# Attention and mixture of experts on one core: another order of the block products of experts 1 to 7, with old and new layer-2 steps among them

## The chip, the cores and the metric

The kernel runs on one core of a Trainium2 chip. The metric is the device time of one execution in microseconds (us), median over runs.

## The reference

An attention (8 batches, 8 heads, 576 positions, head width 64; scores below the row's maximum less tau are masked out) gives 4608 rows x of 512 numbers. They go to a mixture of 8 experts:

```python
logits = x @ w_gate
noisy_logits = logits + np.log1p(np.exp(x @ w_noise)) * noise
top2 = np.argpartition(-noisy_logits, 2, axis=1)[:, :2]
...                                    # top2_w: softmax over the two logits
for e in range(E):
    for k in range(2):
        mask = top2[:, k] == e
        h = np.maximum(x[mask] @ w1[e], 0.0)
        out[mask] += top2_w[mask, k, None] * (h @ w2[e])
```

w1 is 8 x 512 x 1024, w2 is 8 x 1024 x 512, all fp32.

## The kernel before

Attention and routing fill the first part, with expert 0's first two groups of tokens among them. This document is about what follows, `run` (L1370): expert 0's third group, then experts 1 to 7, each of at most 1188 tokens in two halves, `phase(e, 0, ...)` with 640 tokens and `phase(e, 1, ...)` with 548.

Every matmul is done in three, since both operands are split into a rounded part and a rest (hi and lo, both fp32r): hi x hi, hi x lo, lo x hi. Each split costs a rounding on ScalarE (hi) and a subtract on VectorE (lo).

**Layer 1 of a half** is computed in 28 block products instead of 32, by the scheme that multiplies 2x2 blocks with seven products. For each of four units u (two of the eight blocks of the hidden width) there are the products k = 1 to 7; the 28 pairs (k, u) stand in the table `STEPS`. A product (`product`, L1216) is six matmuls of 320 columns in half 0 and of 274 in half 1. The sums of weight blocks that the scheme needs are four additions on GpSimd (`w1sum`, L1103), those of the inputs are on VectorE (`xsum`, L1177). Products go to PSUM banks x (one of two, by u), y and z. `evict` (L1240) empties them: k = 1, 5, 6 a copy on ScalarE (L1248) to one of three SBUF tiles; k = 2, 3, 7 an add on VectorE to that tile (L1251), then a relu on ScalarE one step later (L1255) and a subtract on VectorE two steps later (L1256); k = 4 relu and subtract from the bank itself. Products 1, 6, 4 and 7 of a unit use the same bank x, so that each of them waits for the eviction of the one before.

**Layer 2 of a half** is built by `second_steps` (L1349) from steps of three matmuls. `plain` (L1293) is a tile of 128 tokens in eight steps of 128x512; its output is scaled by the gate into one of three y buffers (L1301, on VectorE) and scattered (L1019, on GpSimd). `wide2` (L1314) is the rest of half 1 (292 columns) in four quarters of eight steps: VectorE transposes a quarter from its bank (L1333), and after the fourth multiplies by the gates (L1337); ten scatters of 32 rows follow. Layer-2 steps use two PSUM banks in turn. Half 0 has five plain tiles, half 1 two and the wide block (in expert 7 five). Expert 0's third group has one plain tile and a wide block as well.

**The order** is written out by hand. `step` issues the matmuls of one step, then evictions that are due, then side work: `run` gives each piece of side work the number of the step that it goes behind, in a list for the products and one for the layer-2 steps. Each engine runs its instructions in that order. SyncE issues the weight loads (`w1load` L1098, `w2load` L1125), GpSimd the gathers of token rows (`gather2`), which are bounced through DRAM (`bounce2`), loaded as blocks (`load2`) and transposed on VectorE (`turn2`, L1175); `sums` then schedules the input sums (L1186), roundings (`xhi` L1205, ScalarE) and subtracts (`xlo` L1210). Weights are split by `w1hi` (L1118) and `w1lo` (L1122), `w2hi` (L1132) and `w2lo` (L1137). Four raw buffers (`q`) take the loads of both layers' weights. Layer-1 weights of units 0 and 1 for the next half 0 are split in half 1, those of units 2 and 3 at the head of half 0; all eight layer-2 weights are loaded and split in half 0. One scatter at most is issued after each step.

The steps of a half before:

```python
steps = first[:-1] + second[:4] + first[-1:] + second[4:]   # L1359
```

27 products, four layer-2 steps, product (4, 3), and the other layer-2 steps.

## Time and profile before

| | |
|---|---|
| time, median of 3 runs | 1633.54 us (1632.52 to 1637.58) |
| the profiled execution | 1635.43 us, span 1633.3 us |
| TensorE matmul (PE) | 1464.0 us, 90% |
| VectorE (DVE) | 1095.3 us, 67% |
| ScalarE (ACT) | 822.0 us, 50% |
| GpSimd (POOL) | 761.3 us, 47% |

Busy times are of the profiled execution. Matmuls overlap in the pipeline, so a row's duration is longer than its distance to the next one. The program's part of this document starts at 713.67 us with the wide block of expert 0; expert 1 starts at 741.61, and the last matmul is at about 1623 us. The names in the rows are of memory places (n_xr, n_p and so on), which are used by several buffers; the line tells which operation it is.

### The profile page before, as it was taken

To read this page: it belongs to the slowest core of one execution; us is meant where nothing else is said; L and a number is where in the kernel's file an instruction comes from. 1 tells how busy PE (TensorE), PEld (TensorE's weight loads), DVE (VectorE), ACT (ScalarE), POOL (GpSimd) and SP (SyncE) were. 2 spreads that over 40 slices of the span, in tenths; PEclk is the share of its full clock that TensorE was granted. 3 is DMA by queue.
4 is the path that set the end of the run, shared out by engine and by line. 5 is a ranking of instruction groups with operands and counts; after the bars stand their busy time and mean duration, and the time that the engine had idled before them with its cause. 6 is when DMAs were issued, how large, how long until landed. Compare 5 with 4: busy or idle time off the path is not lost. (4 is left out here: it accounts for less than half of the span.)

```text
span 1633.3 us, 27794 instructions
## 1 busy us (share of the span) xinstructions
PE 1464.0 (90%) x9086; PEld 1190.4 (73%) x9086; DVE 1095.3 (67%) x2879; ACT 822.0 (50%) x1727; POOL 761.3 (47%) x1129
## 2 busy tenths in 40 slices
...
GB/s 184 172 208 184 213 161 207 163 222 175 200 168 149 202 128 81 104 146 132 72 160 98 84 163 90 90 167 55 122 152 70 122 155 63 130 143 62 141 33 28
DMA packets 189281, 220.59 MB, mean 135 GB/s; under 512 B 64212, under 2 KB 112300, under 8 KB 188112
## 3 DMA queue, kind: packets, MB, share of 16 engines
...
## 5 line engine op out<-in xcount | busy, mean ns | idle before, releaser
L1019 POOL DMA_INDIRECT out<-n_y,sx x52 | 85.8, 1650 | 366.6 <-DVE n_y L1301 362.6
L295 ACT ACTIVATE e<-ns,nm 128x576 f32<-128x576 f32 x288 | 223.2, 775 | 40.6 <-DVE ns L293 37.6
L318 DVE SCALAR_TENSOR_TENSOR p<-ns,thr,e 128x576 f32<-128x576 f32 x256 | 223.3, 872 | 21.2 <-ACT thr L303 20.4
L293 DVE TENSOR_SCALAR_CACHE_REDUCE ns<-sp 128x576 f32<-128x576 f32 x288 | 214.3, 744 | 22.2 <-PE sp L282 18.0
L330 PEld LDWEIGHTS tp<-ident,p 128*128 128x128 f32 x1024 | 110.6, 144 | 99.5 <-ACT ot L402 23.1
L333 ACT ACTIVATE pt<-tp 128x512 f32<-128x512 f32 x256 | 151.1, 590 | 56.3 <-PE tp L330 55.3
L396 PE MATMUL tp<-pt,vt 128*64 128x256 f32 (+1 forms) x1024 | 176.5, 429 | 0.0
L330 PE MATMUL tp<-ident,p 128*128 128x128 f32 x1024 | 167.7, 286 | 0.0
L282 PE MATMUL sp<-ks,qh 128*128 128x288 f32 x496 | 159.6, 335 | 4.6 <-DVE ns L293 4.6
L1248 ACT ACTIVATE n_qr<-m_tp 128x320 f32<-128x320 f32 (+1 forms) x168 | 67.7, 407 | 164.8 <-DVE n_y L1301 84.3
L1232 PE MATMUL m_tp<-n_vt,n_pt 128*128 128x320 f32 (+1 forms) x364 | 96.2, 319 | 48.3 <-ACT n_qr L1248 41.6
L282 PE MATMUL sp<-ks,ql 128*128 128x288 f32 x496 | 138.4, 296 | 0.6 <-DMA ql<-loq 0.6
L1019 POOL DMA_INDIRECT out<-n_y,ix x60 | 97.7, 1629 | 82.7 <-DVE n_y L1337 68.2
L1232 PE MATMUL m_tp<-n_p,n_pt 128*128 128x274 f32 (+1 forms) x700 | 122.0, 313 | 6.2 <-ACT n_qr L1248 4.9
L210 POOL TENSOR_TENSOR lok<-kr,hik 128x640 fp32r<-128x640 f32 x31 | 57.3, 1847 | 139.7 <-ACT hik L209 128.3
L1232 PEld LDWEIGHTS m_tp<-n_p,n_pt 128*128 128x128 f32 x700 | 107.8, 200 | 9.7 <-ACT n_qr L1248 6.7
L1301 DVE TENSOR_SCALAR n_y<-m_sp,gw 128x512 f32<-128x512 f32 (+1 forms) x52 | 39.0, 749 | 108.6 <-PE m_sp L1311 108.6
L1232 PEld LDWEIGHTS m_tp<-n_vt,n_pt 128*128 128x128 f32 x364 | 67.4, 199 | 54.2 <-ACT n_qr L1248 45.2
L1251 DVE TENSOR_TENSOR n_qr<-m_tp,n_qr 128x320 f32<-128x320 f32 (+1 forms) x168 | 76.9, 458 | 42.1 <-PE m_tp L1232 40.8
L639 POOL DMA_INDIRECT slot_table<-pay,sl x80 | 88.2, 1102 | 33.6 <-DVE m_vt L879 16.4
L1205 ACT ACTIVATE n_vt<-n_qr 128x640 fp32r<-128x640 f32 (+1 forms) x42 | 29.5, 701 | 139.3 <-DVE n_qr L1186 139.3
L282 PEld LDWEIGHTS sp<-ks,qh 128*128 128x128 f32 x496 | 93.5, 189 | 6.5 <-DVE ns L293 4.6
...
## 6 DMA issues: line engine op xcount, KB each, us to landing
...
```

Source lines behind the costliest of these rows:

```text
L282: nc.tensor.matmul(o, q_, k_, start=(i == 0), stop=(i == len(parts) - 1))
L293: nc.vector.tensor_scalar(ns, sp[:, :, 0:HALF], -1.0 / math.sqrt(D), None, op0=ALU.mult, op1=ALU.min, accum_out=nm)
L295: nc.scalar.activation(e, ns, AF.Exp, bias=nm, scale=-1.0)
L318: nc.vector.scalar_tensor_tensor(p, ns, thr, e, op0=ALU.is_le, op1=ALU.mult, accum_out=ssum[n][:, c:c + 1])
L330: nc.tensor.transpose(tp[:, kt, :], p[:, 128 * kt:128 * kt + 128], ident)
L333: nc.scalar.activation(pt[n][:, s, :, c0:c0 + 128], tp, AF.Copy)
L396: nc.tensor.matmul(o[64 * s:64 * s + 64, 0:c1 - c0], w, x, start=(kt == 0), stop=(kt == 4))
L639: st = nc.gpsimd.indirect_dma_start(out=table, out_offset=bass.IndirectOffsetOnAxis(ap=d["sl"][0:m, i, c:c + 1], axis=0), in_=d["pay"][0:m ...
L1019: st = self.nc.gpsimd.indirect_dma_start(out=out, out_offset=bass.IndirectOffsetOnAxis(ap=idx, axis=0), in_=y, in_offset=None, compute_op= ...
L1232: nc.tensor.matmul(ps[:, 0:n], w[a[0]][hw][:, 128 * (a[1] + c):128 * (a[1] + c) + 128], s[hx][:, c0 + c, t0:t0 + n], start=(first and i == ...
L1248: return lambda: nc.scalar.activation(to, ps, AF.Copy)
L1251: return lambda: nc.vector.tensor_tensor(to, ps, to, op=ALU.add)
```

## The change

Part by part:

- `STEPS` has another order of the 28 products. Two entries "old" are the last two layer-2 steps of the half before, which are taken off its end and put behind the first and the fourth product. Four entries "new" are the half's own first layer-2 steps, one ahead of product (7, 3) and three ahead of (4, 3). The last tile and the last quarter of a half take the hidden blocks in the order `LASTORDER`.
- A plain tile's output is scaled on ScalarE instead of VectorE. There are four y buffers instead of three.
- For each half, the five gathers go behind steps 1 to 5, into five places instead of three; bounces behind 12 to 16, loads behind 18 and 19, transposes and input sums one to four steps later than before.
- Layer-1 weights of units 0 to 2 of the next expert are split among the products of half 1 (unit 0's sum in half 0's layer-2 part), those of unit 3 in half 1's layer-2 part. The sum of a unit lies in two tiles, so its rounding and its subtract are two instructions each, and go between those of the two weights. Half 0 has no layer-1 weights left, but for expert 1, which keeps units 2 and 3.
- The first four layer-2 weights of experts 2 to 7 are loaded at the end of half 1 of the expert before; all eight are split behind the steps 2, 6, 8, 11, 14, 17, 20 and 23 of half 0.
- A scatter is issued after every third step among the products and every second one behind them.
- In expert 0's third group, side work is put at other steps. Two constant tiles are filled with a copy of another tile's zeros, without a tile of their own.

```diff
-PLACES = 3
+PLACES = 4
-STEPS = ((1, 0), (2, 0), (5, 0), (6, 0), (3, 0), (1, 1), (7, 0), (2, 1), (6, 1), (4, 0), (5, 1), (7, 1),
-         (1, 2), (3, 1), (4, 1), (6, 2), (2, 2), (5, 2), (7, 2), (1, 3), (3, 2), (4, 2), (6, 3), (2, 3), (5, 3), (7, 3),
-         (3, 3), (4, 3))
+LASTORDER = (1, 5, 2, 6, 3, 7, 0, 4)
+STEPS = ((1, 0), "old", (2, 0), (5, 0), (6, 0), "old", (3, 0), (1, 1), (7, 0), (2, 1), (5, 1), (6, 1), (4, 0), (3, 1),
+         (1, 2), (7, 1), (2, 2), (5, 2), (6, 2), (4, 1), (3, 2), (1, 3), (7, 2), (2, 3), (5, 3), (6, 3), (4, 2), (3, 3),
+         "new", (7, 3), "new", "new", "new", (4, 3))
...
-        lay(("S",), "xl", 0, 768)
+        lay(("S", 0), "xl", 0, 512)
+        lay(("S", 1), "nz", 0, 256)
...
     def w1hi(self, e, u, n):
         if e < E:
-            self.nc.scalar.activation(self.buf("W", u, n, 0, dtype=F32R), self.w1part(e, u, n), AF.Copy)
+            for hi, _, x in self.w1part(e, u, n):
+                self.nc.scalar.activation(hi, x, AF.Copy)
...
-        return self.buf("R0", i % 3) if (e, p) == (1, 0) else self.buf("H", *((3, 0), (3, 1), (7, 0))[i % 3])
+        return self.buf("R0", i % 3) if (e, p) == (1, 0) else self.buf("H", *((3, 0), (3, 1), (6, 0), (7, 0), (7, 1))[i])
...
-            nc.vector.tensor_scalar(y[0:m].rearrange("p (j c a) -> p c j a", j=4, c=4),
-                                    ps[0:m].rearrange("p (c j a) -> p c j a", c=4, j=4), gw[0:m, t:t + 1], None,
-                                    op0=ALU.mult)
+            nc.scalar.activation(y[0:m].rearrange("p (j c a) -> p c j a", j=4, c=4),
+                                 ps[0:m].rearrange("p (c j a) -> p c j a", c=4, j=4), AF.Copy, scale=gw[0:m, t:t + 1])
...
-        steps = first[:-1] + second[:4] + first[-1:] + second[4:]
+        steps, new = [], []
+        for x in STEPS:
+            if x == "old":
+                steps.append(self.old.pop(0) if self.old else (lambda: None, []))
+            elif x == "new":
+                new.append(len(steps))
+                steps.append(second[len(new) - 1])
+            else:
+                steps.append(((lambda k=x[0], u=x[1]: self.product(p, k, u)), self.evict(p, *x)))
+        first = len(steps)
+        steps += second[len(new):]
+        if (e, p) != (E - 1, 1):
+            self.old = steps[-2:]
+            del steps[-2:]
...
-            self.store(1 if len(steps) - i > 2 else 0)
+            if i % 3 == 2 if i < first else i % 2:
+                self.store(1)
...
+            if e == 1:
+                s = split1(e, 2, (0, 1, 2)) + sum1(e, 3, 3) + split1(e, 3, (6, 7, 8)) + [
+                    (a, call(self.w2load, e, i)) for i, a in enumerate((4, 4, 9, 9))]
+                v = (9, 11, 14, 16, 19, 21, 24, 26)
+            else:
+                s, v = [], (2, 6, 8, 11, 14, 17, 20, 23)
             self.phase(
                 e, 0,
-                rows(e, 1, (2, 5, 8, 12, 16), (7, 10, 13, 17, 21), (11, 14)) + split1(e, 2, 0)
-                + [(3, call(self.w2load, e, 0)), (4, call(self.w2load, e, 1))] + sum1(e, 3, 3) + split1(e, 3, 5)
-                + [(9 + i, call(self.w2load, e, 2 + i)) for i in range(2)]
-                + [(9 + 2 * i, call(self.w2hi, e, i)) for i in range(8)] + [(10 + 2 * i, call(self.w2lo, e, i)) for i in range(8)]
-                + [(11 + 2 * i, call(self.w2load, e, 4 + i)) for i in range(4)] + turns(e, 1, (18, 22), (18, 22)),
-                turns(e, 1, (1, 3, 9), (1,), 2) + sums(e, 1, 13) + [(4, call(self.tokens, n, 0)), (30, call(self.index, n, 0))])
+                rows(e, 1, (1, 2, 3, 4, 5), (12, 13, 14, 15, 16), (18, 19)) + s
+                + [(a, call(self.w2hi, e, i)) for i, a in enumerate(v)] + [(a + 1, call(self.w2lo, e, i)) for i, a in enumerate(v)]
+                + [(a + 2, call(self.w2load, e, 4 + i)) for i, a in enumerate(v[:4])] + turns(e, 1, (25, 27), (26, 29)),
+                turns(e, 1, (5, 7, 13), (6,), 2) + sums(e, 1, 14) + [(4, call(self.tokens, n, 0)), (30, call(self.index, n, 0))]
+                + [(2, call(self.w1load, n, 0)), (8, call(self.w1load, n, 1))] + sum1(n, 0, 20))
             self.phase(
                 e, 1,
-                rows(n, 0, (2, 5, 8, 12, 16), (7, 10, 13, 17, 21), (11, 14)) + [(8, call(self.w1load, n, 0)),
-                (14, call(self.w1load, n, 1))] + sum1(n, 0, 14) + split1(n, 0, 16) + [(20, call(self.w1load, n, 2))]
-                + turns(n, 0, (18, 22), (18, 22)) + sum1(n, 1, 21) + split1(n, 1, 24),
-                turns(n, 0, (1, 3, 9), (1,), 2) + sums(n, 0, 11) + [(3, call(self.w1load, n, 3))] + sum1(n, 2, 32))
+                rows(n, 0, (1, 2, 3, 4, 5), (12, 13, 14, 15, 16), (18, 19)) + split1(n, 0, (9, 10, 13)) + sum1(n, 1, 12)
+                + [(16, call(self.w1load, n, 2))] + split1(n, 1, (17, 18, 20)) + [(22, call(self.w1load, n, 3))]
+                + sum1(n, 2, 22) + split1(n, 2, (25, 26, 28)) + sum1(n, 3, 30) + turns(n, 0, (25, 27), (26, 29)),
+                turns(n, 0, (5, 7, 13), (6,), 2) + sums(n, 0, 14) + split1(n, 3, (4, 5, 6))
+                + [(a, call(self.w2load, n, i)) for i, a in enumerate((8, 9, 14, 15))])
```

How the instructions move, at three places. The line numbers of the changed kernel are up to 7 higher for `product` and `evict` (L1232 is L1239, L1248 is L1255, L1255 is L1262), 7 for the roundings (L1118 is L1125, L1132 is L1139, L1205 is L1212), and the tile output is L1308.

TensorE at the head of half 0 of expert 4. Before, the products (1, 0), (2, 0) and (5, 0) follow each other:

```order
L1232 MATMUL m_tp_9745<-n_p 128x320 x2
L1232 MATMUL m_tp_9745<-n_p,n_xr_9999 128x320
L1232 MATMUL m_tp_9745<-n_p 128x320 x2
L1232 MATMUL m_tp_9745<-n_p,n_xr_9999 128x320
L1232 MATMUL m_tp_9779<-n_p 128x320 x2
L1232 MATMUL m_tp_9779<-n_p,n_xr_9999 128x320
L1232 MATMUL m_tp_9779<-n_p 128x320 x2
L1232 MATMUL m_tp_9779<-n_p,n_xr_9999 128x320
L1232 MATMUL m_tp_9797<-n_p 128x320 x2
L1232 MATMUL m_tp_9797<-n_p,n_pt_10009 128x320
L1232 MATMUL m_tp_9797<-n_p 128x320 x2
L1232 MATMUL m_tp_9797<-n_p,n_pt_10009 128x320
```

Now, with the last steps of expert 3's wide block (L1332) in the first rows:

```order
L1332 MATMUL m_sp_9033<-n_e_10158,n_e_10456 128x292
L1332 MATMUL m_sp_9033<-n_e_10159,n_ns_10440 128x292
L1239 MATMUL m_tp_9744<-n_p 128x320 x2
L1239 MATMUL m_tp_9744<-n_p,n_xr_9938 128x320
L1239 MATMUL m_tp_9744<-n_p 128x320 x2
L1239 MATMUL m_tp_9744<-n_p,n_xr_9938 128x320
L1332 MATMUL m_sp_9033<-n_qh_10145,n_pt_9953 128x292
L1332 MATMUL m_sp_9033<-n_qh_10145,n_pt_10166 128x292
L1332 MATMUL m_sp_9033<-n_qh_10146,n_pt_9953 128x292
L1239 MATMUL m_tp_9784<-n_p 128x320 x2
L1239 MATMUL m_tp_9784<-n_p,n_xr_9938 128x320
L1239 MATMUL m_tp_9784<-n_p 128x320 x2
```

A step of the old wide quarter stands between the first product and the second.

ScalarE at the same place. Before, from the last input rounding (L1205) on, the layer-1 weights' roundings (L1118) stand among the copies (L1248) and relus (L1255) of the first products:

```order
L1205 ACTIVATE n_vt_10006<-n_qr_9794 128x640
L1118 ACTIVATE n_pt_10162<-n_raw_9760 128x512
L1248 ACTIVATE n_qr_9794<-m_tp_9745 128x320
L1118 ACTIVATE n_pt_10162<-n_raw_9777 128x512
L1255 ACTIVATE n_qh_10141<-n_qr_9794 128x320
L1118 ACTIVATE n_pt_10162<-n_xl 128x768
L1248 ACTIVATE n_qr_9988<-m_tp_9797 128x320
L1248 ACTIVATE n_qr_9794<-m_tp_9745 128x320
L1255 ACTIVATE n_qh_10141<-n_qr_9794 128x320
L1118 ACTIVATE n_xr_10153<-n_hik_9952 128x512
L1248 ACTIVATE n_qr_9794<-m_tp_9762 128x320
L1118 ACTIVATE n_xr_10153<-n_lok_9954 128x512
```

Now, from the last input rounding (L1212) on:

```order
L1212 ACTIVATE n_vt_10035<-n_qr_9759 128x640
L1255 ACTIVATE n_qr_9759<-m_tp_9744 128x320
L1139 ACTIVATE n_pt_9953<-n_raw_9765 128x512
L1262 ACTIVATE n_qh_10145<-n_qr_9759 128x320
L1255 ACTIVATE n_qr_9761<-m_tp_9801 128x320
L1255 ACTIVATE n_qr_9759<-m_tp_9744 128x320
L1139 ACTIVATE n_ks_10153<-n_raw_9767 128x512
L1262 ACTIVATE n_qh_10145<-n_qr_9759 128x320
L1255 ACTIVATE n_qr_9759<-m_tp_9769 128x320
L1139 ACTIVATE n_pt_10166<-n_hik_9946 128x512
L1262 ACTIVATE n_ptr_10147<-n_qr_9761 128x320
L1262 ACTIVATE n_ql_10149<-n_qr_9759 128x320
```

The roundings of layer-1 weights are gone from there, and layer-2 weights (L1139) have come forward, one for about every three evictions.

ScalarE in the products of half 1 of expert 4. Before, copies and relus only:

```order
L1248 ACTIVATE n_qr_9794<-m_tp_9745 128x274
L1255 ACTIVATE n_qh_10141<-n_qr_9794 128x274
L1248 ACTIVATE n_qr_9988<-m_tp_9797 128x274
L1248 ACTIVATE n_qr_9794<-m_tp_9745 128x274
L1255 ACTIVATE n_qh_10141<-n_qr_9794 128x274
L1248 ACTIVATE n_qr_9794<-m_tp_9762 128x274
L1255 ACTIVATE n_ptr_10143<-n_qr_9988 128x274
L1255 ACTIVATE n_ql_10145<-n_qr_9794 128x274
L1248 ACTIVATE n_qr_9794<-m_tp_9762 128x274
L1255 ACTIVATE n_ptr_10143<-m_tp_9745 128x274
L1248 ACTIVATE n_qr_9988<-m_tp_9797 128x274
```

Now:

```order
L1255 ACTIVATE n_qr_9759<-m_tp_9744 128x274
L1308 ACTIVATE n_y_10534<-m_sp_9033,gw_75 128x4x4x32
L1262 ACTIVATE n_qh_10145<-n_qr_9759 128x274
L1255 ACTIVATE n_qr_9759<-m_tp_9769 128x274
L1262 ACTIVATE n_ptr_10147<-n_qr_9761 128x274
L1125 ACTIVATE n_p<-n_raw_9765 128x512
L1262 ACTIVATE n_ql_10149<-n_qr_9759 128x274
L1125 ACTIVATE n_p<-n_xl 128x512
L1125 ACTIVATE n_p<-n_nz 128x256
L1255 ACTIVATE n_qr_9761<-m_tp_9801 128x274
L1255 ACTIVATE n_qr_9759<-m_tp_9769 128x274
L1262 ACTIVATE n_ptr_10147<-m_tp_9744 128x274
```

A tile output of half 0 (L1308) and the layer-1 roundings of the next expert (L1125) stand among the evictions.

## Rows read from the trace of the kernel before

**Rows 1.** The page: the span, and part 1, busy us, share of the span and number of instructions of each engine.

```profile
span 1633.3 us, 27794 instructions
...
PE 1464.0 (90%) x9086; PEld 1190.4 (73%) x9086; DVE 1095.3 (67%) x2879; ACT 822.0 (50%) x1727; POOL 761.3 (47%) x1129
```

**Rows 2.** A table of stretches (stretch in us from the span's start, its length, busy us and instructions of PE, PEld, DVE, ACT and POOL, then TensorE's granted clock, the DMA engines' share and GB/s; the line that begins with sum adds up the busy us, and for an engine that is never idle the length). The first line is the sum over seven stretches: the 36 layer-2 steps after the last product of half 0 in experts 1 to 7. The other two are of the first 27 products of half 1: that of expert 7 alone, and the sum over experts 1 to 7, where the first number is the seven lengths added.

```profile
sum 174.76, PE 174.76 PEld 141.97 DVE 87.10 ACT 32.45 POOL 46.93; mean PE 24.97 PEld 20.28 DVE 12.44 ACT 4.64 POOL 6.70
...
1574.00:1594.73 20.73, 20.73 (x163) 20.67 (x162) 11.14 (x25) 9.38 (x26) 1.60 (x2) 1.00 0.11 13
sum 170.13, PE 151.56 PEld 145.76 DVE 99.94 ACT 83.11 POOL 79.83; mean PE 21.65 PEld 20.82 DVE 14.28 ACT 11.87 POOL 11.40
```

**Rows 3.** The time line of PE in expert 3 (start us, us, engine, line, operation, out<-in, tile, count): a product of half 0 and the start of the next one; two quarters of the wide block.

```profile
1000.15 1.04 PE L1232 MATMUL m_tp<-n_p,n_pt 128*128 128x320 f32 x6
1001.03 0.31 PE L1232 MATMUL m_tp<-n_vt,n_pt 128*128 128x320 f32 x1
...
1102.78 0.56 PE L1326 MATMUL m_sp<-n_qh,n_pt 128*128 128x292 f32 x3
...
1106.01 0.68 PE L1326 MATMUL m_sp<-n_qh,n_pt 128*128 128x292 f32 x3
```

**Rows 4.** The table of stretches again, columns as in rows 2. The first 27 products of half 0: expert 1, expert 3, and the sum over experts 1 to 7. The wide block of half 1, sum over experts 1 to 6. The wide block of expert 0.

```profile
741.61:782.23 40.62, 28.91 (x165) 26.71 (x163) 24.74 (x52) 17.96 (x39) 25.55 (x25) 0.92 0.62 150
...
992.45:1034.95 42.50, 28.45 (x164) 26.35 (x163) 24.88 (x52) 17.80 (x39) 25.95 (x25) 0.89 0.62 146
...
sum 291.82, PE 207.02 PEld 191.64 DVE 173.65 ACT 124.97 POOL 180.03; mean PE 29.57 PEld 27.38 DVE 24.81 ACT 17.85 POOL 25.72
...
sum 111.13, PE 88.76 PEld 87.12 DVE 68.58 ACT 25.43 POOL 36.42; mean PE 14.79 PEld 14.52 DVE 11.43 ACT 4.24 POOL 6.07
...
713.67:741.61 27.94, 15.65 (x97) 14.95 (x96) 20.87 (x43) 9.03 (x14) 12.21 (x14) 0.88 0.35 102
```

**Rows 5.** The time line of PE in the products of half 0 of expert 3; in brackets at the end the idle time before the instruction and what ended it.

```profile
1018.48 0.63 PE L1232 MATMUL m_tp<-n_vt,n_pt 128*128 128x320 f32 x1 [4.83 <-ACT n_qr L1248]
```

**Rows 6.** The waits of PE from expert 1 on, by what was waited for: us in total, times, longest us.

```profile
PE m_tp L1232 <- ACT n_qr L1248: 94.2, 53, 4.8
PE m_sp L1326 <- DVE n_y L1333: 22.4, 6, 4.6
...
PE m_sp L1311 <- DVE n_e L1256: 2.8, 4, 0.9
```

**Rows 7.** The time line of ACT in the same products, the roundings of layer-2 weights (L1132) that waited for a DMA.

```profile
1017.47 0.63 ACT L1132 ACTIVATE n_pr<-n_lok 128x512 fp32r<-128x512 f32 x1 [5.96 <-DMA n_lok<-w]
...
1024.22 0.63 ACT L1132 ACTIVATE n_ot<-n_raw 128x512 fp32r<-128x512 f32 x1 [1.42 <-DMA n_raw<-w]
...
1028.90 0.63 ACT L1132 ACTIVATE n_ql<-n_hik 128x512 fp32r<-128x512 f32 x1 [2.43 <-DMA n_hik<-w]
...
1031.82 0.63 ACT L1132 ACTIVATE n_ns<-n_lok 128x512 fp32r<-128x512 f32 x1 [1.63 <-DMA n_lok<-w]
```

**Rows 8.** The time line of SP's queue there: two issues of layer-2 weight loads (L1128), for the rounding at 1017.47 and the one at 1024.22.

```profile
1013.36 0.37 SPq L1128 DMA_DIRECT2D n_lok<-w  x1
...
1016.16 0.35 SPq L1128 DMA_DIRECT2D n_raw<-w  x1
```

**Rows 9.** The time lines of PE and DVE in half 1 of expert 3: the step after product (4,0), and the last operation on that product's bank.

```profile
1071.90 0.92 PE L1232 MATMUL m_tp<-n_p,n_pt 128*128 128x274 f32 x6
...
1072.53 0.44 DVE L1256 SCALAR_TENSOR_TENSOR n_ptr<-m_tp,n_ptr 128x274 fp32r<-128x274 f32 x1 [0.50 <-ACT n_ptr L1255]
```

**Rows 10.** The time line of DVE where half 0 of expert 4 begins: transposes and gate products of the last wide quarter, and a subtract of a layer-1 weight.

```profile
1122.33 0.64 DVE L1333 STREAM_TRANSPOSE n_y<-m_sp 128x128 f32<-128x128 f32 x3 [2.59 <-PE m_sp L1326]
1122.90 1.59 DVE L1337 TENSOR_TENSOR n_y<-n_y,ti 128x512 f32<-128x512 f32 x3
...
1125.40 0.68 DVE L1122 TENSOR_TENSOR n_pt<-n_raw,n_pt 128x512 fp32r<-128x512 f32 x1
```

**Rows 11.** The time lines of DVE and POOL in the wide block of expert 3: input sums of 128x320 (L1186), input subtracts of 128x640 (L1210), and one of the additions of a weight sum on POOL (L1111).

```profile
1103.18 0.48 DVE L1186 TENSOR_TENSOR n_qr<-n_loq,n_kr 128x320 f32<-128x320 f32 x1
...
1105.87 0.81 DVE L1210 TENSOR_TENSOR n_p<-n_kr,n_p 128x640 fp32r<-128x640 f32 x1
1106.60 0.82 DVE L1210 TENSOR_TENSOR n_p<-n_hiq,n_p 128x640 fp32r<-128x640 f32 x1
...
1108.94 1.01 DVE L1186 TENSOR_TENSOR n_qr<-n_hiq,n_qr 128x320 f32<-128x320 f32 x1
...
1109.68 0.86 POOL L1111 TENSOR_TENSOR n_raw<-n_raw 128x256 f32<-128x256 f32 x1
```

**Rows 12.** The time lines of DVE and PE in the wide block of expert 0: the tile output, and the starts of the second and of the third quarter.

```profile
719.49 0.71 DVE L1301 TENSOR_SCALAR m_y<-m_sp,gw 128x512 f32<-128x512 f32 x1
...
720.25 0.67 PE L1326 MATMUL m_sp<-m_qh,m_pt 128*128 128x292 f32 x3 [3.23 <-DVE m_y L1301]
...
731.25 1.10 PE L1326 MATMUL m_sp<-m_qh,m_pt 128*128 128x292 f32 x3 [7.52 <-DVE m_y L1333]
```

**Rows 13.** The time line of POOL in expert 3: two scatters of wide blocks at the start of half 0, and a gather (L1148) of half 1.

```profile
1005.33 1.60 POOL L1019 DMA_INDIRECT out<-n_y,ix  x1 [0.16 <-issue]
...
1007.23 1.62 POOL L1019 DMA_INDIRECT out<-n_y,ix  x1 [0.27 <-issue]
...
1068.57 0.99 POOL L1148 DMA_INDIRECT n_xr<-x_rows,sx  x1 [0.30 <-PE m_tp L1232]
```

More of the change, by code (lines that the diff above doesn't have):

```diff
@@ L245, in attention @@
     QD = [work.tile([128, 128], F32R, name=f"qd{i}") for i in range(2)]
[L246 to L247 removed]
     for t in QD:
[L249 removed]
+        nc.vector.tensor_copy(t, xl.rearrange("p a b -> p (a b)"))
     st = {}
```

55 lines of the change are left out of this document (29 added, 26 removed).

## The prediction, made before the changed kernel was run

> **What bounds the kernel now.** I read the page first, then a table of stretches, then TensorE's waits, then the time lines of expert 3. On the page TensorE is busy for 1464.0 us of a span of 1633.3 us and the other engines for two thirds or less [rows 1], so the end is set by TensorE's own work and by what keeps it waiting. The change touches nothing before the third group of expert 0, so the question is what TensorE loses from there on.
>
> The stretches show where. The 36 layer-2 steps that follow the products of half 0 run at TensorE's pace in all seven experts (174.76 us, busy all the time: 24.97 us each, 0.69 us a step) [rows 2]. Half 1 of the last expert, with no work for a next expert beside it, does its first 27 products in 20.73 us, 0.77 us each [rows 2]. In half 0 a product takes 0.88 us when nothing waits (1000.15 to 1001.03) [rows 3], so 27 of them need 23.8 us; they take 291.82 us over seven experts, 41.7 us each [rows 4]. The same products of half 1 take 149.4 us in experts 1 to 6 (170.13 less 20.73) [rows 2], 24.9 us each: 4.2 us lost. The wide block needs 3.23 us for a quarter (1102.78 to 1106.01) [rows 3], so 12.9 us, and takes 111.13 / 6 = 18.5 us; in expert 0 it takes 27.94 us [rows 4]. So the largest loss is half 0: 18 us in each expert.
>
> Its cause stands in three time lines. TensorE stands still, here for 4.83 us, until ScalarE's copy of a product (L1248) [rows 5]; such waits are 94.2 us over the seven experts, in 53 places [rows 6]. ScalarE is in order, and what stands ahead of those copies is the rounding of a layer-2 weight that has not landed: 5.96, 1.42, 2.43 and 1.63 us [rows 7]. The weight of the 5.96 us was issued at 1013.36, 4.1 us before it was used; the next took 8 us (1016.16 to 1024.22) [rows 7, 8]. The waits cost twice: TensorE is busy 207.02 / 7 = 29.6 us for work of 23.8, because part of it runs at the lower of its two clock levels (granted 0.89 in expert 3) [rows 4].
>
> **The change part by part.**
> *Half 0, experts 2 to 7.* The layer-1 roundings and GpSimd's sums leave this stretch, the first four layer-2 weights are loaded in the half before, the last four 7 to 10 steps (6 to 9 us) ahead of their rounding, where they had 6 or fewer. The waits above go. What is late next: the bank of product (4,u) is written again by (1,u+2) after one step in between, where it was two and four. ScalarE's relu and VectorE's subtract end 1.12 us after the step in between starts (1071.90 to 1072.97 and 0.05 to start) [rows 9]; that is 0.3 us more than the 0.88 us step (a subtract in half 0 being a little longer). The first time VectorE is also behind: the transposes and products of the last wide quarter, 0.64 and 1.59 us [rows 10], now run inside the products, and with its queue of adds and weight subtracts (0.68) [rows 10] it is some 0.5 us late at that point: 0.8 us. With 0.1 for the rest that is 1.2 us, and I allow 2.0 us for a weight that still lands late (bounds 0, and the 5.5 us that 1.42, 2.43 and 1.63 make now without the longest [rows 7]; nearer the lower, since the loads have 6 to 9 us where the two shown took 4 and 8): 23.8 + 3.2 = 27.0 us. 291.82 - 40.62 - 6 x 27.0 = **89.2 us** [rows 4]. The old steps only move over a border.
> *Half 0 of expert 1* keeps two roundings of layer-1 weights, and its first layer-2 loads are issued 5 steps, 4.4 us, ahead. Its loss lies between the 3.2 us of the others and 3.2 + 2 x 3.6 us, if two loads take 8 us as the one shown; I take 5.5, nearer the lower: 40.62 - 29.3 = **11.3 us**.
> *The wide block, experts 1 to 6.* Its third quarter waits until VectorE has read the first, 22.4 us in six [rows 6]. VectorE was late because GpSimd summed weights beside it: the same 128x320 subtract takes 0.48 us alone and 1.01 us there [rows 11]. That sum leaves the stretch. But tile outputs now stand on ScalarE ahead of the input roundings, so these start only when tile 6 is done: output 0.7 [rows 12], first rounding 0.8 (as long as its subtract), seven subtracts 0.74 apart 5.2 [rows 11], two sums 0.9, last rounding 0.8, the first quarter's transposes 0.64 [rows 10] and 0.1 between, 9.1 us against 6.5 us of two quarters. The wait becomes 2.6 us. The lower clock level costs 1.9 us there now (busy 88.76 / 6 = 14.8 for 12.9) [rows 4]; I take 1.7 us with the shorter wait: 4.3 instead of 5.6 us, 6 x 1.3 = **7.8 us**. The fourth y buffer removes a wait that these seven experts do not show: nothing.
> *The wide block of expert 0.* The 3.23 us wait was for a tile output behind VectorE's transposes of input rows; on ScalarE it is free of them [rows 12]. The 7.52 us wait shrinks to some 2.4 us, since the first quarter's transposes now follow six row sums (719.5 + 6 x 0.40 + 0.64 = 722.5, and two quarters end at 713.67 + 6.46 = 720.1), and the fourth quarter waits behind six subtracts of 0.81, 4.9 us [rows 11, 12]: 12.9 + 7.3 + 1.7 for the clock + 1 for more roundings = 22.9 us, **5.0 us** less [rows 4].
> *Half 1, experts 1 to 6.* Three groups of roundings stand among the products instead of two, and three GpSimd sums instead of two. I take 0.4 us for the bank as in half 0, 0.9 for roundings ahead of copies, 1.6 for one VectorE operation held in each of three sums (0.53 each, 1.01 less 0.48) [rows 11], 1.3 for the rest: 4.2 us, **nothing gained**. Bounds: 1 us, and 10 us if all four adds of each sum hold one.
> *Layer-2 steps after half 1's products*: TensorE's 2.8 us of waits for the last hidden block [rows 6] go, since more steps stand in between: **2.8 us**. The zero tile that goes and the wider gaps between scatters cost nothing: GpSimd is busy 47% [rows 1].
>
> Sum: 89.2 + 11.3 + 7.8 + 5.0 + 0 + 2.8 = 116.1 us. The profiled execution took 1635.43 us, so 1519.3; the median of the runs is 1.9 us below it: **1517 us**.
>
> **The rivals.**
> *Half 1 becomes VectorE's stretch (0.18).* A subtract beside GpSimd's adds takes 1.01 instead of 0.48 us [rows 11]; if all four adds of each of three sums hold one operation so, that is 6.4 us where I count 1.6, so 4.8 us more in each of six halves with 0.6 us of clock: 1517 + 32 = 1549. Against it: VectorE is busy (99.94 - 11.14) / 6 = 14.8 us of 24.9 there now [rows 2]. The Trainium skill (SBUF — State Buffer, "SBUF: two separate sides") speaks for this rival: a VectorE operation with two SBUF inputs and a GpSimd operation that reads SBUF exclude each other for a whole instruction. The stretched subtract agrees with it; by that rule alone half 1 would come out near 1549.
> *Layer-2 weights still land late in half 0 (0.12).* The same transfers now share 27 us instead of 42. If the 5.5 us stay, with 1.7 us of clock, that is 5.2 us more than the 2.0 allowed, in six experts: 1517 + 31 = 1548. Against it: the loads have 6 to 9 us, and one of the two shown took 4.
> *Slower: outputs on ScalarE wait for scatters (0.06).* The fourth output of half 0 needs the buffer whose wide blocks are scattered last, behind five gathers of 1.3 us (0.99 and 0.30 before it) and ten scatters, 46 us after the half began (27, and 28 steps of 0.69). With c us for a scatter that is 6.5 + 10c; ScalarE waits from c = 4.0, and the gain of 19 us an expert is gone from c = 5.9. At 6.5 us a scatter it is 25 us: 6 x 6 us beyond the gain, 1671. The rows have 1.9 us from one to the next [rows 13], and nothing beside them would triple that.
> *The change does not reach the bound (0.04).* If TensorE waits for the eviction chains themselves and ScalarE's queue only happens to end last, half 0 stays as it is: 1632, within 0.3%.
>
> **How the numbers follow.** The forecast has 0.60. Its own bounds (half 0 between 24.5 and 30 us, half 1 between 21.5 and 26, the wide wait between 1 and 4 us) give 1484 to 1545; both rivals of the same sign lie below 1564, which with some of each at once is the upper end. About 0.3% (5 us) is what a measurement of this kernel can tell from no change. Faster: 0.60 + 0.18 + 0.12 = 0.90; same 0.04; slower 0.06.
>
> **What would show it.** In the profile after, the first products of half 0 in experts 2 to 7 should take 26 to 28 us with a granted clock near 1.0, ScalarE's rounding of layer-2 weights should not wait for a DMA there, and TensorE's longest wait there should be on VectorE's subtract, below 1 us. The third quarter of the wide block should still wait 2 to 3 us. Half 1's products should stay near 25 us. Wrong would be: a half 0 above 32 us, a half 1 above 30 us, or outputs on ScalarE that wait for an earlier scatter.

## The result and the profile after

The changed kernel takes 1514.99 us, median of 4 runs (1513.83 to 1521.61); before, beside it, 1633.03 us. The ratio is 0.9288, with a 95% interval from 0.9246 to 0.933. The forecast was 1517 us in a range from 1484 to 1564.

The page of the profile after, to be read against [rows 1]:

```profile
span 1512.1 us, 27923 instructions
...
PE 1424.1 (94%) x9086; PEld 1159.8 (77%) x9086; DVE 1061.1 (70%) x2853; ACT 856.1 (57%) x1808; POOL 754.2 (50%) x1149
```

TensorE is busy 40 us less for the same number of matmuls: part of what it lost before was its lower clock level. The table of stretches after, columns as in [rows 2]: the wide block of expert 0; the first 26 products of half 0 in expert 1, in expert 3, and summed over experts 2 to 7; then sums over experts 1 to 6 of half 1's first 26 products, of the rest up to the wide block (with expert 3's row ahead of it), and of the wide block. Half 0 from expert 2 on and half 1 from expert 1 on also have the two old steps in their stretch of products, and the wide blocks of experts 1 to 6 two steps fewer.

```profile
711.84:738.31 26.47, 15.93 (x98) 15.46 (x96) 17.05 (x40) 8.23 (x13) 8.46 (x9) 0.74 0.31 86
...
738.31:766.26 27.95, 24.17 (x159) 22.85 (x157) 22.35 (x48) 17.53 (x40) 23.71 (x25) 1.00 0.74 195
...
959.07:986.01 26.94, 24.76 (x165) 23.72 (x164) 18.24 (x41) 14.87 (x33) 21.49 (x25) 1.00 0.73 172
...
sum 160.05, PE 148.39 PEld 142.12 DVE 108.98 ACT 89.22 POOL 128.50; mean PE 24.73 PEld 23.69 DVE 18.16 ACT 14.87 POOL 21.42
...
sum 140.95, PE 132.22 PEld 126.47 DVE 98.26 ACT 86.12 POOL 76.14; mean PE 22.04 PEld 21.08 DVE 16.38 ACT 14.35 POOL 12.69
...
1037.22:1053.94 16.72, 14.48 (x63) 11.61 (x61) 12.72 (x36) 4.83 (x11) 4.72 (x7) 0.90 0.38 105
...
sum 98.86, PE 85.36 PEld 68.74 DVE 75.83 ACT 28.95 POOL 28.39; mean PE 14.23 PEld 11.46 DVE 12.64 ACT 4.82 POOL 4.73
...
sum 86.27, PE 75.77 PEld 74.30 DVE 47.66 ACT 31.11 POOL 10.01; mean PE 12.63 PEld 12.38 DVE 7.94 ACT 5.19 POOL 1.67
```

To compare, I take products and steps at the paces of [rows 2, 3] (0.88, 0.77, 0.69 and 0.40 us) and bring each stretch to the same work. The rest of half 1 up to the wide block took this in the kernel before, summed over experts 1 to 6 (16 steps and one product, which need 11.9 us each):

```profile
sum 77.72, PE 74.48 PEld 59.29 DVE 59.26 ACT 17.07 POOL 9.97; mean PE 12.41 PEld 9.88 DVE 9.88 ACT 2.85 POOL 1.66
```

| stretch | before | forecast | after | gain forecast | gain measured |
|---|---|---|---|---|---|
| half 0, 27 products, experts 2 to 7 | 41.9 | 27.0 | 160.05/6 - 0.81 + 0.88 = 26.7 | 89.2 | 90.7 |
| the same, expert 1 | 40.6 | 29.3 | 28.8 | 11.3 | 11.8 |
| wide block, experts 1 to 6 | 18.5 | 17.2 | 86.27/6 + 0.81 = 15.2 | 7.8 | 20.0 |
| wide block, expert 0 | 27.9 | 22.9 | 26.5 | 5.0 | 1.5 |
| half 1, 27 products, experts 1 to 6 | 24.9 | 24.9 | 140.95/6 - 1.39 + 0.77 = 22.9 | 0 | 12.2 |
| half 1, lost between there and the wide block | 77.72/6 - 11.9 = 1.1 | 0.6 | 98.86/6 - 12.64 = 3.8 | 2.8 | -16.5 |
| rest (ahead of expert 0's wide block 1.8) | | | | 0 | 1.5 |
| sum | | | | 116.1 | 121.2 |

The sum came out some 5 us above the forecast, and that is partly luck, because misses cancel: the wide block and half 1's products gave 24 us more than forecast, and a new wait took 19 us back. (12.64 us are 16 steps and two products, 1.39 us two steps, 0.81 us two steps of the wide block.) The waits of TensorE after, from expert 0's wide block on (us in total, times, longest), against [rows 6], which begin with expert 1:

```profile
PE m_tp L1239 <- DVE n_qr L1258: 13.8, 7, 2.3
PE m_tp L1239 <- ACT n_qr L1255: 10.7, 15, 1.5
PE m_sp L1332 <- DVE m_y L1339: 10.5, 2, 9.9
PE m_sp L1332 <- DVE n_y L1339: 10.5, 6, 1.8
...
PE m_tp L1239 <- issue: 4.3, 10, 0.8
```

The 94.2 us on ScalarE's copies became 10.7, and from expert 1 on no rounding of a layer-2 weight (L1139) waits for a DMA. 13.8 us are on VectorE's add (L1258), and most of them are new: 2.2 us at one place in each of six halves. The time lines of DVE, POOL and PE there, in half 1 of expert 3:

```profile
1039.85 0.41 DVE L1258 TENSOR_TENSOR n_qr<-m_tp,n_qr 128x274 f32<-128x274 f32 x1
1040.75 0.89 DVE L1263 SCALAR_TENSOR_TENSOR n_xr<-n_qr,n_xr 128x274 fp32r<-128x274 f32 x1 [0.50 <-ACT n_xr L1262]
1041.57 1.20 DVE L1130 TENSOR_TENSOR n_pt<-n_raw,n_pt 128x512 fp32r<-128x512 f32 x1
1042.69 0.43 DVE L1258 TENSOR_TENSOR n_qr<-m_tp,n_qr 128x274 f32<-128x274 f32 x1
...
1039.79 0.74 POOL L1113 TENSOR_TENSOR n_lok<-n_lok 128x256 f32<-128x256 f32 x1
1040.61 0.73 POOL L1113 TENSOR_TENSOR n_xl<-n_lok,n_hik 128x256 f32<-128x256 f32 x1
1041.42 0.80 POOL L1113 TENSOR_TENSOR n_nz<-n_hik,n_xl 128x256 f32<-128x256 f32 x1
...
1043.18 0.39 PE L1239 MATMUL m_tp<-n_vt,n_xr 128*128 128x274 f32 x1 [2.24 <-DVE n_qr L1258]
```

Product (4,3) writes the bank of (7,3), which VectorE's add at 1042.69 has to empty first. That add stands behind the add of (3,3), a wait for its relu on ScalarE, and two subtracts of 0.89 and 1.20 us that overlap GpSimd's additions; the add at 1039.85, which reads PSUM, keeps 0.41 us beside an addition. In five of six experts the clock level falls in the steps behind this wait (granted 0.90 over expert 3's row above), 1.5 us more; in expert 4 it falls in the wide block.

### The profile page after: what moved, and what is told of

Read it like the earlier page. It is cut to its first block, busy times and chain, and to the rows that moved or that the text cites. A ratio compares the mean times of both kernels' runs of the same rounds, so it can differ in the third digit from the quotient of the medians.

```text
span 1512.1 us, 27923 instructions
## 1 busy us (share of the span) xinstructions
PE 1424.1 (94%) x9086; PEld 1159.8 (77%) x9086; DVE 1061.1 (70%) x2853; ACT 856.1 (57%) x1808; POOL 754.2 (50%) x1149
## 4 chain that ended last, share of the span: by engine, by line
PE 66%; DVE 10%; issue 9%; ACT 6%; DMA 4%; POOL 3%; SPq 1%; POOLq 0%; DVEq 0%; ACTq 0%
PE m_tp L1239 14%; PE m_sp L1317 13%; PE tp L397 11%; PE tp L331 9%; PE sp L283 9%; PE m_sp L1332 3%; PE m_sp L1000 2%; DVE n_pt L1130 2%; PE tp L417 1%; DVE n_p L1217 1%; DVE n_qr L1258 1%; DMA slot_table<-pay,sl 1%; PE tp L416 1%; POOL out L1021 1%; DMA out<-n_y,sx 1%
## 5 line engine op out<-in xcount | busy, mean ns | idle before, releaser
L319 DVE SCALAR_TENSOR_TENSOR p<-ns,thr,e 128x576 f32<-128x576 f32 x256 | 221.8, 866 | 22.6 <-ACT thr L304 20.7
L1021 POOL DMA_INDIRECT out<-n_y,sx x52 | 82.1, 1579 | 243.2 <-ACT n_y L1308 238.0
L1258 DVE TENSOR_TENSOR n_qr<-m_tp,n_qr 128x320 f32<-128x320 f32 (+1 forms) x168 | 77.0, 461 | 115.2 <-PE m_tp L1239 103.7
L1239 PE MATMUL m_tp<-n_p,n_pt 128*128 128x274 f32 (+1 forms) x700 | 117.0, 303 | 12.7 <-ACT n_qr L1255 8.1
L1255 ACT ACTIVATE n_qr<-m_tp 128x320 f32<-128x320 f32 (+1 forms) x168 | 67.7, 411 | 107.0 <-PE m_tp L1239 103.6
L1239 PEld LDWEIGHTS m_tp<-n_p,n_pt 128*128 128x128 f32 x700 | 100.9, 188 | 19.4 <-ACT n_qr L1255 11.3
L1308 ACT ACTIVATE n_y<-m_sp,gw 128x512 f32<-128x512 f32 (+1 forms) x52 | 35.5, 685 | 130.2 <-PE m_sp L1317 102.7
L640 POOL DMA_INDIRECT slot_table<-pay,sl x80 | 88.2, 1102 | 33.7 <-DVE m_vt L881 16.5
L283 PEld LDWEIGHTS sp<-ks,ql 128*128 128x128 f32 x496 | 94.4, 190 | 0.0
L1239 PE MATMUL m_tp<-n_vt,n_pt 128*128 128x320 f32 (+1 forms) x364 | 89.4, 301 | 4.4 <-issue 3.3
L397 PEld LDWEIGHTS tp<-pt,vt 128*64 128x64 f32 x1024 | 56.7, 135 | 42.4 <-issue 27.8
```

The lines of the kernel that those rows point to most:

```text
L283: nc.tensor.matmul(o, q_, k_, start=(i == 0), stop=(i == len(parts) - 1))
L319: nc.vector.scalar_tensor_tensor(p, ns, thr, e, op0=ALU.is_le, op1=ALU.mult, accum_out=ssum[n][:, c:c + 1])
L397: nc.tensor.matmul(o[64 * s:64 * s + 64, 0:c1 - c0], w, x, start=(kt == 0), stop=(kt == 4))
L640: st = nc.gpsimd.indirect_dma_start(out=table, out_offset=bass.IndirectOffsetOnAxis(ap=d["sl"][0:m, i, c:c + 1], axis=0), in_=d["pay"][0:m ...
L1021: st = self.nc.gpsimd.indirect_dma_start(out=out, out_offset=bass.IndirectOffsetOnAxis(ap=idx, axis=0), in_=y, in_offset=None, compute_op= ...
L1239: nc.tensor.matmul(ps[:, 0:n], w[a[0]][hw][:, 128 * (a[1] + c):128 * (a[1] + c) + 128], s[hx][:, c0 + c, t0:t0 + n], start=(first and i == ...
```

## The experiments

Two things have to be known to read them. They ran in three groups, each on a chip of its own with the kernel before beside it: order_old, order_only, loads_late and round_half0; change_again, tail_sum and tail_dve; rows_only, wide_sum, out_dve and tail_both. I compare times inside a group; the third has no changed kernel in it, so that its runs can be set beside one only by their ratios and stages. And the part ahead of expert 0's wide block, which is the same in the changed kernel, change_again, tail_sum and tail_dve, ended at 711.8 to 718.9 us in their profiles, so stretches tell more than totals.

**Control.** The changed kernel once more:

> The changed kernel as it is, to stand beside the other runs of this call on the same chip. The run loads_late turned out to have the same order of instructions on every engine as the changed kernel (nothing stands between the two places of the loads in SyncE's queue), and took 1504 us where the changed kernel had taken 1515: if that is the chip, this run may lie anywhere from 1502 to 1522.

1519.88 us (1518.89 to 1520.83), ratio 0.9258 (0.9229 to 0.9287). It is the control of tail_sum and tail_dve; for order_old, order_only and round_half0 the control is loads_late, whose edit did nothing:

```diff
-                s, v = [], (2, 6, 8, 11, 14, 17, 20, 23)
+                s, v = [(i, call(self.w2load, e, i)) for i in range(4)], (2, 6, 8, 11, 14, 17, 20, 23)
...
-                + [(a, call(self.w2load, n, i)) for i, a in enumerate((8, 9, 14, 15))])
```

> The changed kernel with the first four layer-2 weights of experts 2 to 7 loaded behind steps 0 to 3 of half 0 instead of at the end of the half before; everything else stays. Queue theory: the first rounding stands behind step 2, some 1.5 us after its load is issued, and a load takes 4 to 8 us, so ScalarE waits 3 to 6 us there and TensorE's copy with it, with 1 to 2 us of lower clock behind it: 4 to 7 us in each of six experts, 1540 to 1557. If the loads' place does not matter (the first copies have slack), 1513 to 1520.

1504.45 us (1502.2 to 1504.84), ratio 0.9169 (0.9109 to 0.9229). Between the old and the new place of these loads SyncE has nothing else to issue, so its order, and that of every other engine, is the changed kernel's. A step number orders work on its own engine; it does not hold an idle queue back. Both expected times are void.

**One part alone: the places of gathers, bounces and input loads**, in half 0, with the change's five landing places instead of three.

```diff
-                rows(e, 1, (2, 5, 8, 12, 16), (7, 10, 13, 17, 21), (11, 14)) + split1(e, 2, 0)
+                rows(e, 1, (1, 2, 3, 4, 5), (12, 13, 14, 15, 16), (18, 19)) + split1(e, 2, 0)
...
-                ... turns(e, 1, (18, 22), (18, 22)), turns(e, 1, (1, 3, 9), (1,), 2) + sums(e, 1, 13)
+                ... turns(e, 1, (25, 27), (26, 29)), turns(e, 1, (5, 7, 13), (6,), 2) + sums(e, 1, 14)
```

> The kernel before with one part of the change, in half 0 alone: gathers of the next half behind steps 1 to 5 into five places, bounces behind 12 to 16, loads, transposes and input sums at the change's steps. Products, roundings, weight loads and outputs stay. Queue theory, one link further back: in the kernel before SyncE issues a layer-2 load behind a bounce that waits for its gather (292.8 us of waits in 33 places), so ScalarE's rounding waits for the weight and TensorE for the copy. With the bounces behind all but the last loads TensorE's waits on the copy fall from 94 to below 50 us and half 0 from 41.7 us by 6 to 12: 1545 to 1600. If the loads are late because their buffers come free late or transfers take long, less than 20 us: 1620 to 1640.

1577.45 us, ratio 0.9622 (0.9599 to 0.9645). The waits of SyncE's queue for gathers (us, times, longest), in the kernel before:

```profile
SPq L1157 <- DMA n_xr<-x_rows,sx: 292.8, 33, 29.7
```

and in rows_only:

```profile
SPq L1157 <- DMA n_xr<-x_rows,sx: 158.1, 6, 27.0
```

27 of 33 are gone; the six that are left are one for each half 1, which this run doesn't touch. TensorE's waits on the copy in rows_only:

```profile
PE m_tp L1232 <- ACT n_qr L1248: 68.5, 35, 5.6
```

and the 27 products of half 0, summed over seven experts:

```profile
sum 238.66, PE 184.60 PEld 178.42 DVE 159.35 ACT 119.52 POOL 179.65; mean PE 26.37 PEld 25.49 DVE 22.76 ACT 17.07 POOL 25.66
```

34.1 instead of 41.7 us each. So one link further back than the prediction went: GpSimd's gather stood behind scatters and a weight sum, SyncE's bounce waited for it, and the next layer-2 load stood behind the bounce. In the kernel before, in expert 3, the gather and the bounce ahead of the load that was issued at 1013.36 [rows 8] are:

```profile
1009.16 1.39 POOL L1148 DMA_INDIRECT n_xr<-x_rows,sx  x1 [0.30 <-issue]
...
1012.93 0.33 SPq L1157 DMA_DIRECT2D stage<-n_xr  x1
```

Half 0's fall of 7.6 us is as expected; the waits fell less (68.5, not below 50). Layer-1 roundings are still there, which may be why.

One more run on the kernel before put the roundings and subtracts of the last five layer-2 weights two steps later and left their loads where they were; 1565 to 1595 us were expected. It took 1679.81 us (1677.51 to 1682.42), ratio 1.0231 (1.0197 to 1.0265). In it the eighth weight is loaded into the buffer of the fourth ahead of the fourth's subtract, so what it computes is not this layer, and VectorE's subtract waits for that load, 106.4 us in seven places. TensorE's waits on the copies fell as expected, to 49.6 us; 98.6 us on VectorE's adds came in their place. Its time says nothing about the change.

**One part alone: the order of the products**, with old and new steps:

```diff
-STEPS = ((1, 0), (2, 0), (5, 0), (6, 0), (3, 0), (1, 1), ...
+STEPS = ((1, 0), "old", (2, 0), (5, 0), (6, 0), "old", (3, 0), (1, 1), ...      # all of the changed table
```

> The kernel before with the new table of products and its old and new steps, and nothing else of the change. Queue theory: the roundings of layer-1 weights and of late layer-2 weights still stand ahead of the copies, so half 0 stays at 39 to 43 us for its 27 products and the time at 1615 to 1645. Order theory: half 0 falls to 30 us or less, the time is below 1570.

1600.22 us, ratio 0.9747 (0.9682 to 0.9813): between the two. Half 0 (26 products and, from expert 2 on, two old steps), over seven experts:

```profile
sum 253.86, PE 192.20 PEld 181.54 DVE 164.57 ACT 122.06 POOL 182.08; mean PE 27.46 PEld 25.93 DVE 23.51 ACT 17.44 POOL 26.01
```

TensorE's waits in order_only:

```profile
PE m_tp L1235 <- DVE n_ns L1259: 38.9, 14, 5.1
PE m_tp L1235 <- DVE n_qr L1254: 26.6, 17, 2.2
PE m_tp L1235 <- ACT n_qr L1251: 21.2, 18, 4.3
```

The order moves most of the waits from the copies to VectorE's subtracts and adds, and half 0 falls to 35 us from expert 2 on, not to 30. Half 1's products fall here too, from 24.9 us to 23.6 with two steps more.

**The opposite: the change without its order of products.**

```diff
-STEPS = ((1, 0), "old", (2, 0), ...
+STEPS = ((1, 0), (2, 0), (5, 0), ... (5, 3), (7, 3), (3, 3), "new", "new", "new", "new", (4, 3))   # before's order
-        if (e, p) != (E - 1, 1):
-            self.old = steps[-2:]
-            del steps[-2:]
```

> The changed kernel with the table of products of the kernel before: no old steps, the four new steps together ahead of (4,3); loads, roundings, sums, outputs and scatters stay where the change put them. Queue theory (what stood ahead of the copies on ScalarE made half 0 slow, the order of the products little): half 0 of experts 2 to 7 stays below 30 us for its products, the time is 1510 to 1545. Order theory (the distance between two uses of a bank decides): half 0 goes back towards 35 to 40 us, the time is above 1570. The wait of 2.2 us for VectorE's add ahead of product (4,3) in half 1 should shrink, since three steps more stand between them.

1495.63 us (1494.11 to 1496.31), ratio 0.9117 (0.9057 to 0.9176), 9 us below the changed kernel of its group (loads_late); from expert 0's wide block to the last matmul it takes 766.9 us, where loads_late takes 781.5. The 27 products of half 0, experts 2 to 7, in order_old:

```profile
sum 148.34, PE 144.81 PEld 142.43 DVE 111.36 ACT 84.51 POOL 116.48; mean PE 24.14 PEld 23.74 DVE 18.56 ACT 14.09 POOL 19.41
```

24.7 us each, and no wait ahead of (4,3). The changed kernel in that group, loads_late (26 products, two old steps):

```profile
sum 150.74, PE 146.38 PEld 141.94 DVE 108.54 ACT 88.63 POOL 127.26; mean PE 24.40 PEld 23.66 DVE 18.09 ACT 14.77 POOL 21.21
```

25.2 us for the same work. Once the roundings no longer wait, the new order brings nothing in half 0, and with three steps between (7,3) and (4,3) instead of five (two less, not three as the expectation says) it makes the new wait. This is the fastest kernel of all, and it has none of the order that the change is named after.

**The layer-1 roundings of units 2 and 3 in half 0**, as in expert 1, for all experts:

```diff
-            if e == 1:
+            if True:
...
-                + sum1(n, 2, 22) + split1(n, 2, (25, 26, 28)) + sum1(n, 3, 30) + turns(n, 0, (25, 27), (26, 29)),
+                + sum1(n, 2, 22) + turns(n, 0, (25, 27), (26, 29)),
```

> The changed kernel with the schedule that the change gives to expert 1's half 0 in all experts: the layer-1 weights of units 2 and 3 split in half 0, the layer-2 loads issued there. Queue theory: half 0 loses 2 us more, as expert 1 does (27.95 against 26.19 to 26.96 us with two steps more), 6 x 2 = 12 us; in half 1 a sum, its roundings and subtracts leave the end of the products, so that the 2.2 us wait ahead of product (4,3) and the 1.5 us of lower clock behind it go, 6 x 3.7 = 22 us: 1500 to 1510. If expert 1's loss is only that of its start and the wait ahead of (4,3) has another cause than VectorE's queue, 1515 to 1530.

1500.57 us, ratio 0.9154 (0.9093 to 0.9214), where the control has 1504.45. The time is in the expected range, but it is only 4 us below its control, where the expectation counts 22 us won and 12 lost. Both signs are as expected: half 0 takes 27.8 us where that control has 25.1, and the wait ahead of (4,3) is gone (4.33 us for two products and four steps that need 4.3).

**The new wait**, first by taking a weight subtract out of VectorE's queue:

```diff
-split1(n, 2, (25, 26, 28))
+split1(n, 2, (25, 26, 31))
```

> The changed kernel with one rounding and subtract of a layer-1 weight (unit 2's last) moved from ahead of VectorE's add of product (7,3) to behind it, GpSimd's sum where it was. Queue theory: the add comes 1.1 to 1.2 us earlier, the wait ahead of (4,3) falls from 2.24 to 1.0 to 1.2 us: 6 to 15 us less than the changed kernel on the same chip. If the wait is set by something other than what stands ahead of the add on VectorE, it stays at 2.2 us.

1510.96 us against 1519.88, ratio 0.9201 (0.9164 to 0.9238); TensorE's waits on L1258 in tail_dve:

```profile
PE m_tp L1239 <- DVE n_qr L1258: 7.4, 8, 1.1
```

1.1 us each instead of 2.3, and the layer-2 steps behind take 8.3 us where the control's take 9.9. With the transposes moved too:

```diff
-turns(n, 0, (25, 27), (26, 29))
+turns(n, 0, (25, 30), (26, 30))
```

> The run tail_dve with one thing more: the transposes of the second block of rows in half 1 are moved behind VectorE's add of product (7,3) too. Queue theory: 0.95 us of transposes leave the queue ahead of the adds of (3,3) and (7,3), so that of the wait of 1.0 us that was left ahead of (4,3) 0.1 us or nothing remains: 4 to 8 us less than tail_dve, 12 to 22 less than the changed kernel, 1488 to 1505. If the add of (3,3) and its relu set the wait whatever stands ahead, as tail_dve.

1507.24 us (1503.03 to 1513.61), ratio 0.92 (0.9174 to 0.9227): just above what was expected, and the ratio is that of tail_dve. Its waits:

```profile
PE m_tp L1239 <- issue: 9.3, 11, 1.7
...
PE m_tp L1239 <- DVE n_qr L1258: 1.9, 6, 0.3
```

The add costs 0.3 us now, as queue theory has it. From the wide block of expert 0 to the end it takes 787.0 us, tail_dve 790.5, change_again 804.4 (both on another chip). But TensorE waits 9.3 us for nothing that the profile shows, all in half 0, so the products take 27.8 us there, 0.9 us more than in tail_dve; that takes back what the add gave.

**Does GpSimd hold VectorE?** The first try moved its sum behind a step where GpSimd had nothing between:

```diff
-+ sum1(n, 3, 30)
...
-split1(n, 3, (4, 5, 6))
+sum1(n, 3, 4) + split1(n, 3, (4, 9, 10))
```

> The changed kernel with GpSimd's sum of unit 3's layer-1 weights moved from behind the step after product (7,3) of half 1 to the first layer-2 step after the products, and unit 3's second and third rounding 4 steps later. If VectorE's operations there are held by GpSimd's adds (a subtract of 0.89 instead of 0.44, a weight subtract of 1.20 instead of 0.68), both return to their length, the wait of 2.24 us ahead of product (4,3) falls to 1.0 to 1.4 us, and with it some of the lower clock behind it: 6 to 15 us less than the changed kernel on the same chip. If it is only VectorE's queue that is long, nothing changes: within 3 us.

1518.95 us against 1519.88; the sum ran where it had run, and the wait stayed 2.26 us: no answer, for the same reason as loads_late. The second put it behind a scatter (`sum1(n, 3, 17)`, the roundings at 32 to 34, two layer-2 loads at 38 and 39):

> The changed kernel with GpSimd's sum of unit 3's layer-1 weights behind the scatter of tile 6, so that it runs in the wide block of half 1 (in the run tail_sum it did not move: nothing stood between the two places in GpSimd's queue); unit 3's roundings behind the third quarter. If GpSimd's adds hold VectorE's operations: at the end of the products the subtract falls from 0.89 to 0.44 us and the weight subtract from 1.20 to 0.68, the wait of 2.24 us ahead of (4,3) to about 1.2; in the wide block the input sums and subtracts are stretched as in the kernel before and the third quarter waits 3 to 4.5 us instead of 1.75. The time then stays within 10 us of the changed kernel. If GpSimd does not matter, both waits stay as they are.

1539.48 us, ratio 0.9381 (0.9361 to 0.94): more than 10 us above the changed kernel by either control. TensorE's waits in wide_sum:

```profile
PE m_sp L1332 <- DVE n_y L1339: 26.9, 6, 4.5
...
PE m_tp L1239 <- DVE n_qr L1258: 8.9, 7, 1.4
```

and the time lines of DVE and POOL, first at the end of half 1's products, then in the wide block:

```profile
1055.18 0.45 DVE L1263 SCALAR_TENSOR_TENSOR n_xr<-n_qr,n_xr 128x274 fp32r<-128x274 f32 x1 [0.50 <-ACT n_xr L1262]
1055.70 0.69 DVE L1130 TENSOR_TENSOR n_pt<-n_raw,n_pt 128x512 fp32r<-128x512 f32 x1
...
1070.13 1.36 DVE L1217 TENSOR_TENSOR n_p<-n_kr,n_p 128x640 fp32r<-128x640 f32 x1
...
1074.76 0.81 DVE L1217 TENSOR_TENSOR n_p<-n_loq,n_p 128x640 fp32r<-128x640 f32 x1
...
1070.89 1.20 POOL L1113 TENSOR_TENSOR n_xl<-n_lok,n_hik 128x256 f32<-128x256 f32 x1
```

Ahead of (4,3) the two subtracts are back at 0.45 and 0.69 us and the wait at 1.4; in the wide block input subtracts in a row take 1.34 to 1.36 us beside GpSimd's additions (0.81 without), and the third quarter waits 4.5 us instead of 1.75. So GpSimd's additions do hold VectorE, at both places; that the time would stay within 10 us was wrong. The Trainium skill (SBUF — State Buffer, "SBUF: two separate sides") says that a VectorE operation with two SBUF inputs and a GpSimd operation that reads SBUF lock each other out for a whole instruction. These rows agree in kind: side by side the subtract takes 1.36 us for 0.81, and the addition 1.20 us, where the one at 1040.61 above took 0.73.

**Outputs back on VectorE.**

```diff
-            nc.scalar.activation(y[0:m]..., ps[0:m]..., AF.Copy, scale=gw[0:m, t:t + 1])
+            nc.vector.tensor_scalar(y[0:m]..., ps[0:m]..., gw[0:m, t:t + 1], None, op0=ALU.mult)
```

> The changed kernel with the tile outputs back on VectorE, nothing else. If the outputs ahead of the input roundings on ScalarE set the third quarter's wait of 1.75 us, it falls by about 0.5 us, and the time by 0 to 6 us. If the move to ScalarE is what shortened that wait from 3.7 us, it goes back above 3 us and the time rises by 12 to 25 us, half of it by the clock. VectorE has 0.75 us more in half 1's products for the old tile's output: up to 4 us.

1513.11 us, ratio 0.9229 (0.92 to 0.9258), between those of loads_late and change_again; the third quarter waits 12.2 us in six experts instead of 10.5, so that neither expectation for it came. What the move is worth can't be told from the totals. Half 1's stretch of products takes 24.1 us here in experts 1 to 6, in loads_late 22.8, in change_again 23.6.

## Why the prediction was right, point by point

*Half 0, experts 2 to 7* was right in its cause, and in its size (90.7 for 89.2) partly by luck. Rows_only shows half of the cause by itself. The prediction took the late loads from issue to landing; that SyncE issued them late, behind bounces, it did not see. Of the 3.2 us that it added to 23.8, no layer-2 weight landed late where 2.0 us were allowed (by the step numbers the last four loads are 9 or 10 steps ahead of their rounding, not 7 to 10), and the reused bank cost 0.56 and 0.16 us where 0.8 and 0.3 were counted. What filled most of the rest are two waits that it did not have, in the time line of PE after, in expert 3:

```profile
968.78 0.41 PE L1239 MATMUL m_tp<-n_vt,n_pt 128*128 128x320 f32 x1 [0.82 <-issue]
...
971.45 1.14 PE L1239 MATMUL m_tp<-n_p,n_pt 128*128 128x320 f32 x6 [0.64 <-ACT n_qr L1255]
973.15 1.15 PE L1239 MATMUL m_tp<-n_p,n_pt 128*128 128x320 f32 x6 [0.56 <-DVE n_ptr L1263]
```

The last row is the reused bank, (1,2) behind (4,0). The first, (6,1), has no visible releaser; the second is (3,1), on the copy of (5,1) in another bank. Loads_late, the same order of instructions, has neither and takes 25.2 us for 27 products instead of 26.7.

*Half 0 of expert 1* (11.8 for 11.3) was right in size, for another reason than the one given: no layer-2 load is late there. ScalarE's rounding of a layer-1 weight waits for GpSimd's sum, and TensorE waits 1.03 us for the copy behind it. In the time line of ACT after:

```profile
747.57 0.63 ACT L1125 ACTIVATE n_xr<-n_xl 128x512 fp32r<-128x512 f32 x1 [1.83 <-POOL n_xl L1113]
```

*The wide block*: the step "the wait becomes 2.6 us, with 1.7 us for the clock" was too high twice. The third quarter starts 8.35 us after the first, where 9.1 were counted, so the wait is 1.75; and behind it the clock stayed at its upper level in five of six experts. The last input rounding, which the sum has with 0.8 us of its own, runs beside a subtract, in the time lines of DVE and ACT after:

```profile
1059.98 0.81 DVE L1217 TENSOR_TENSOR n_p<-n_loq,n_p 128x640 fp32r<-128x640 f32 x1
...
1060.09 0.74 ACT L1212 ACTIVATE n_vt<-n_qr 128x640 fp32r<-128x640 f32 x1 [1.50 <-DVE n_qr L1193]
```

Wide_sum shows that GpSimd's sum, which the change took away, made the long wait; with the outputs on VectorE again (out_dve) it is 2.0 us.

*The wide block of expert 0*: "some 2.4 us" became 9.95, in the time lines of DVE and PE after:

```profile
720.82 0.50 DVE L1182 STREAM_TRANSPOSE n_kr<-n_zeros 128x128 f32<-128x128 f32 x2 [4.64 <-DMA n_zeros<-stage]
...
722.54 1.01 DVE L1193 TENSOR_TENSOR n_qr<-n_hiq,n_kr 128x320 f32<-128x320 f32 x1
...
728.36 1.10 PE L1332 MATMUL m_sp<-m_qh,m_pt 128*128 128x292 f32 x3 [9.95 <-DVE m_y L1339]
```

The row sums were to end at 722.5. The last rows landed only at 720.8, and the sums beside GpSimd's additions took up to 1.01 us where 0.40 were counted: the first quarter's transposes came at 727.7.

*Half 1's products*: "nothing gained" failed; they gained 2.0 us each. Of the 4.2 us that were kept as lost, 2.1 are left; in expert 3 TensorE waits 0.77 us for a subtract and 0.26 us for a copy, so the terms for roundings ahead of copies (0.9) and for held VectorE operations (1.6) were too high together. The rival of VectorE as the bound didn't come there. Either half of the change brings the gain: order_only has 22.9 us for 27 products, order_old 22.6. Why either is enough is not shown.

*The steps behind them*: "since more steps stand in between, 2.8 us" failed. The prediction looked at the last hidden block and not at product (4,3), which the new table puts two steps sooner behind (7,3), whose bank it writes. It is the first rival's mechanism at another place: VectorE's queue, held by GpSimd, 2.2 us and 1.5 us of clock in each half.

*The slower rival* fell: ScalarE's outputs name an earlier scatter four times, 4.9 us each, but that is the pace of the tiles (8 steps of 0.69 less the output's 0.69), and TensorE waited 1.0 us for an output once.

Of the signs that were named ahead, half 0's length and clock and the roundings without a wait for a DMA came as told. The third quarter's 2 to 3 us, the 25 us of half 1's products and a longest wait of half 0 on VectorE's subtract did not.
